# Both batch pairs of a delta-rule attention issued together on TensorE, the second into the other half of PSUM

## The chip, the cores and the metric

The kernel runs on one core of a Trainium2 chip. The metric is the device time of one execution in microseconds (us). Engines are named as in the profile: PE is TensorE (PEld its weight loads), DVE is VectorE, ACT is ScalarE, POOL is GpSimd, SP is SyncE, which only issues DMAs here.

## The reference

An attention with a delta rule, followed by two MLPs on its output. B = 4 batches, H = 8 heads, S = 768 tokens, D = 48.

```python
k_n = k / (norm(k) + 1e-06)
for t in range(S):
    y[:, :, t] = q_t @ state
    v_old = state^T k_t
    state = state + beta_t * outer(k_t, v_t - v_old)
x = y rearranged to 3072 tokens x 384
x = relu(x @ w_in)**2 @ w_out             # d_ff 2048, "MoE1"
x = (silu(x @ w_gate) * (x @ w_val)) @ w_out2   # d_ff 1536, "MoE2"
```

All is float32 (the kernel's large products use a high and a low part in fp32r, three products for one).

## The kernel before

Tokens go in six steps J of 128 tokens of all four batches; a step has two chunks c of 64 tokens. The four batches are two pairs p, and the two batches a of a pair lie on the two halves of the 128 partitions. Within a chunk the recurrence is solved in closed form. The pieces, each a small block of fp32 matmuls for one chunk and one pair, are (with the name of the PSUM tile in the profile):

- gram (`ps_g`, L387/L388): k k^T, 64x64 for each head and batch. From it, masked and scaled by beta on DVE (L457, L458), comes the triangular matrix M, which SP sends to DRAM (`m_out`, L465) and loads back in another layout (`tload`, L470). POOL then inverts 32x32 blocks of it in place, in the tile T (`inv`, L512 and L519), some 40 us for a step. SP sends the result out (`nout`, L546) and back (`nback`, eight DMAs, L561).
- t11, m1, m2 (`tq`, `ps_m`, `ps_x`): the off-diagonal block of the inverse, from transposes on DVE (L612) and two products of 32x32 blocks.
- agram (`ps_a`): q k^T, masked on DVE (L498). ks (`ps_k`): the old state times k, subtracted from V on DVE (L646). u (`ps_u`): the inverse times that. ku (`ps_s`): the change of state. y (`ps_y`, L676/L679): the output, copied by ACT into `ys` (L685).

A matmul of float32 runs as two passes, so a block of 8 heads and 2 batches is 32 matmuls in the trace. The two batches of a pair use the tiles (rows 0-63, columns 0-63) and (rows 64-127, columns 64-127) of TensorE, or, where the layout of the keys makes it so, the two others; two of the four 64x64 tiles are in use at a time, and in m1 and m2 two 32x32 tiles.

Norms of the keys: squares on POOL for the later steps (`sq`, L356), sums on DVE (L360), then a chain of eight small DVE operations (`root`, L371 to L378) that gives `nB`; V is multiplied by it on POOL (`vn`, L319). `v` loads V by SP.

After the attention of step 0, MoE1 of step J runs together with the attention of step C = J + 1. MoE1 of a step is a list of half-slots: nine 128x512 matmuls into `ps_h` (L862), then nine into `ps_y` (L888), and so on. Function `plan(C, P)` names for each of 32 half-slots which pieces of the attention of step C, and which gram pieces of the next step P, follow it; `slot` runs what is due. So the order on PE and on SP is the program's order. DVE's order during MoE1 is the program's order too. On POOL and ACT the compiler's scheduler chooses the order at build time, from when it thinks operands will be there. All engines execute in order. The sum of MoE1 (`ye`) goes to DRAM through DMAs that POOL issues (`y_scr`, L905). MoE2 follows, with no attention beside it.

PSUM: three banks hold MoE1's sums (`ps_a`), two its `ps_h`, and three (`ps_t`) all small blocks of the attention. Tile `xr` has two buffers, shared by M and `ys`; V has two buffers.

Of the kernel before, what the change touches and what calls it, by code (L numbers as in the profile page):

```python
# [8 lines left out]
F32 = mybir.dt.float32  # L9
# [12 lines left out]
def delta_attention_moe_moe2_kernel(  # L22
# [361 lines left out]
    def gram_mm(J, c, p, ps):  # L384
        kt = KT[J, c][:, p]
# [22 lines left out]
    def m0(J, c, p):  # L408
        m = MS[J, c, p]
        nc.vector.scalar_tensor_tensor(out=m, in0=g0.pop((J, c, p)), scalar=-1.0, in1=m, op0=ALU.mult, op1=ALU.mult)  # L410
# [37 lines left out]
    def gram(J, c, p, pool=False):  # L448
        ps = ps_t.tile([128, 8, 64], F32, tag="t", name="ps_g")
        gram_mm(J, c, p, ps)  # L450
        m = ap.tile([128, 8, 64], F32, tag="xr", bufs=XR, name="M")
        mk = mask.unsqueeze(1).to_broadcast([128, 8, 64])
        if pool:
            nc.scalar.activation(out=m, in_=ps, func=ACTF.Copy, scale=-1.0)
            nc.gpsimd.tensor_tensor(m, m, mk, op=ALU.mult)
        else:
            nc.vector.scalar_tensor_tensor(out=m, in0=ps, scalar=-1.0, in1=mk, op0=ALU.mult, op1=ALU.mult)  # L457
        (nc.gpsimd if pool else nc.vector).tensor_tensor(  # L458
            m, m, bB[:, 2 * J + c, p, :].unsqueeze(2).to_broadcast([128, 8, 64]), op=ALU.mult
        )  # L460
        MS[J, c, p] = m
# [27 lines left out]
    def a_mask(J, c, p, eng=None):  # L489
        ps, cs = amm.pop((c, p)), slice(c * 64, (c + 1) * 64)  # L490
        for a in range(2):
            pr = slice(64 * a, 64 * a + 64)
            aq, mk = AQ[p][pr, a, :, cs], mask[pr].unsqueeze(1).to_broadcast([64, 8, 64])
            if eng:
                nc.scalar.activation(out=aq, in_=ps[pr], func=ACTF.Copy)
                eng.tensor_tensor(aq, aq, mk, op=ALU.mult)
            else:
                nc.vector.tensor_tensor(aq, ps[pr], mk, op=ALU.mult)  # L498

    def invert(J, part, parts, eng, pr=slice(0, 128)):  # L500
# [4 lines left out]
        for kk in rows[30 * part // parts:30 * (part + 1) // parts]:  # L505
# [91 lines left out]
    def tr11(J, c, p):  # L597
        t = TD[0][:, p] if J == 0 and c else ap.tile([128, 8, 32], F32, tag="tq", bufs=2, name="tq")
        if J == 0:
            ps = bank(p, [128, 8, 32], "ps_tq")  # L600
            for h in range(8):
                for b0 in (0, 64):
                    nc.tensor.matmul(
                        ps[b0:b0 + 32, h], ND[b0:b0 + 32, 16 * c + 8 * p + h], ident[b0:b0 + 32, b0:b0 + 32],
                        start=True, stop=True,
                    )
            for b0 in (0, 64):
                copy(b0 // 64, t[b0:b0 + 32], ps[b0:b0 + 32])
            t11[c, p] = t
            return  # L610
        for b0 in (0, 64):
            nc.vector.transpose(out=t[b0:b0 + 32], in_=NT[c][p][b0:b0 + 32, :, 0:32])  # L612
        t11[c, p] = t

    def merge1(J, c, p):
        ps = bank(p, [128, 8, 32], "ps_m")
        t = t11[c, p]
        n = NT[c][p]
        for h in range(8):
            for b0 in (0, 64):  # L620
                nc.tensor.matmul(ps[b0 + 32:b0 + 64, h], n[b0:b0 + 32, h, 32:64], t[b0:b0 + 32, h], start=True, stop=True)  # L621
        for b0 in (32, 96):
            copy(b0 // 64, t[b0:b0 + 32], ps[b0:b0 + 32])

    def merge2(J, c, p):
        ps = bank(p, [128, 8, 32], "ps_x")
        n = NT[c][p]
        qq = t11.pop((c, p))
        for h in range(8):
            for b0 in (0, 64):  # L630
                r = slice(b0 + 32, b0 + 64)
                b_ = n[r, h, 32:64] if J else ND[r, 16 * c + 8 * p + h]
                nc.tensor.matmul(ps[b0:b0 + 32, h], qq[r, h], b_, start=True, stop=True)  # L633
        for b0 in (0, 64):
            copy(b0 // 64, n[b0:b0 + 32, :, 32:64], ps[b0:b0 + 32])


    def ks(J, c, p):
        if J == 0 and c == 0:
            return  # L640
        ps = bank(p, [128, 8, 48], "ps_k")
        kt = KT[J, c][:, p]
        for h in range(8):
            nc.tensor.matmul(ps[0:64, h], kt[64:112, h], RS[p][64:112, 0, h], start=True, stop=True)  # L644
            nc.tensor.matmul(ps[64:128, h], kt[0:48, h], RS[p][0:48, 1, h], start=True, stop=True)
        nc.vector.tensor_tensor(VT[J, c][:, p], VT[J, c][:, p], ps, op=ALU.subtract)  # L646

    def uu(J, c, p):
        ps = bank(p, [128, 8, 48], "ps_u")
        for h in range(8):  # L650
            for b0 in (0, 64):
                nc.tensor.matmul(  # L652
                    ps[b0:b0 + 64, h], NT[c][p][b0:b0 + 64, h], VT[J, c][b0:b0 + 64, p, h], start=True, stop=True
                )
        for a in range(2):
            pr = slice(64 * a, 64 * a + 64)
            nc.vector.tensor_tensor(
                RS[p][pr, a], ps[pr], bB[pr, 2 * J + c, p, :].unsqueeze(2).to_broadcast([64, 8, D]), op=ALU.mult
            )

    def ku(J, c, p):
        pk = bank(p, [128, 8, 48], "ps_s")
        for h in range(8):
            nc.tensor.matmul(pk[64:112, h], KB[J, c][0:64, p, h], RS[p][0:64, 0, h], start=True, stop=True)  # L664
            nc.tensor.matmul(pk[0:48, h], KB[J, c][64:128, p, h], RS[p][64:128, 1, h], start=True, stop=True)
        return pk

    def state(p, pk):
        nc.vector.tensor_tensor(RS[p][64:112, 0], RS[p][64:112, 0], pk[64:112], op=ALU.add)
        nc.vector.tensor_tensor(RS[p][0:48, 1], RS[p][0:48, 1], pk[0:48], op=ALU.add)  # L670
# [73 lines left out]
    def do_ku(J, c, p):  # L744
        if (J, c) != (NJ - 1, 1):
            pks[J, c, p] = ku(J, c, p)

        if (J, c) == (0, 0):
            state(p, pks.pop((J, c, p)))

    def do_y(J, c, p):
# [15 lines left out]
        "amm": (lambda J, c, p: a_gram(J, c, p, split=True), 0.8), "amask": (a_mask, 0),  # L767
# [14 lines left out]
    def plan(C, P, pool=(), gram_at=(8, 11, 14, 16), agram_at=(3, 6), norm_at=NRM, t11_at=3, nback_at=4):  # L782
# [8 lines left out]
        for p in range(2):  # L791
            at(0, ("ks", C, 0, p))
            at(t11_at, ("t11", C, 0, p))
            at(5, ("m1", C, 0, p))
            at(7, ("m2", C, 0, p))
            at(agram_at[p], ("agram", C, 0, p))
            at(U0[p], ("u", C, 0, p))
            at(K0[p], ("ku", C, 0, p))
            at(Y0[p], ("y", C, 0, p))
            at(KS1[p], ("ks", C, 1, p))  # L800
            at(15, ("t11", C, 1, p))
            at(18, ("m1", C, 1, p))
# [476 lines left out]
```

## Time and profile before

| what | value |
|---|---|
| three runs | 1131.73, 1134.98, 1136.25 us, median 1134.98 |
| span of the profiled execution, first to last instruction | 1128.7 us |
| PE busy | 1061.7 us, 94% of the span |
| DVE, ACT, POOL busy | 610.4, 381.0, 232.4 us |
| start and attention of step 0, then MoE1 of step 0 with C = 1 | 0 to 215 us |
| MoE1 with the attention of C = 2, 3, 4 | three stretches of about 100 us, to 519 us |
| rest of MoE1 with C = 5, MoE1 of the last step | to 690 us |
| MoE2 | 690 to 1128.7 us |

The profiled execution's own time is given by its span; the median of the runs is 6.3 us above it. Busy times are a share of the whole and average over stages with different limits, so the rows further down go by stage.

### The profile page before, as it was taken

Reading aid. Unit: us, or ns where it says so; the run is one execution under the profiler, and the core shown is the slowest. Engines: PE = TensorE matmul, PEld = TensorE weight load, DVE = VectorE, ACT = ScalarE, POOL = GpSimd, SP = SyncE. Lnnn points to the kernel's source line nnn. Section 1 sums busy time; section 2 is a strip of 40 time slices with the busy share of each in tenths; the row PEclk is TensorE's granted clock in tenths of the full one; section 3 lists DMA queues with packets and bytes.
Section 4 is the critical chain, followed back from the end, with each engine's and each line's share of the span. In section 5 each row is a group of like instructions: output and inputs, shape, how many; then the busy total and the mean of one; then the engine's idle time right before and its main releaser. Section 6 shows DMA issues by size and latency. Waiting matters only on the chain.

```text
span 1128.7 us, 24358 instructions
## 1 busy us (share of the span) xinstructions
PE 1061.7 (94%) x10591; PEld 881.4 (78%) x10591; DVE 610.4 (54%) x1026; ACT 381.0 (34%) x683; POOL 232.4 (21%) x367
## 2 busy tenths in 40 slices
PE   5478879999999999999999999999999999999998
PEld 4376767878888887888888787888888888888887
DVE  5777977465475557545443799333343343333333
ACT  2224744322342233234234786222122121221212
POOL 4258005810851381085000000000000000000000
PEclk8567979999999999999999999999999999999999
DMA  9455304533162353324101565001010010100000
GB/s 298 159 148 155 80 21 100 125 88 86 44 154 56 65 122 90 72 44 106 31 17 57 196 224 168 1 1 56 1 56 1 1 56 1 56 1 1 29 1 28
DMA packets 116922, 84.50 MB, mean 75 GB/s; under 512 B 91472, under 2 KB 95440, under 8 KB 116816
## 3 DMA queue, kind: packets, MB, share of 16 engines
q1 hardware_dynamic: 115616, 77.97, 25.3%
q0 software_dynamic: 1056, 4.72, 1.1%
q8 instruction: 83, 1.36, 0.5%
q10 hardware_dynamic: 144, 0.26, 0.1%
q14 instruction: 23, 0.19, 0.1%
HBM read 61.70 MB, written 21.23 MB: 73 GB/s over the span
## 4 chain that ended last, share of the span: by engine, by line
PE 80%; DVE 8%; issue 3%; POOL 3%; DMA 3%; ACT 2%; SPq 0%; DVEq 0%; POOLq 0%; ACTq 0%
PE ps_h L862 15%; PE ps_y L888 15%; PE ps_o L980 13%; PE ps_g L955 13%; PE ps_v L955 13%; PE ps_u L652 2%; PE ps_g L387 2%; PE ps_a L480 2%; POOL T L519 1%; PE ps_k L644 1%; POOL TMP L512 1%; PE ps_m L621 1%; PE ps_y L676 1%; PE ps_x L633 1%; PE ps_s L664 1%
## 5 line engine op out<-in xcount | busy, mean ns | idle before, releaser
L862 PE MATMUL ps_h<-xh,w 128*128 128x512 f32 (+1 forms) x636 | 204.6, 382 | 3.7 <-DVE w L209 3.1
L888 PE MATMUL ps_y<-hh,w 128*128 128x512 f32 (+1 forms) x606 | 156.0, 393 | 0.0
L955 PE MATMUL ps_g<-x2h,w 128*128 128x512 f32 x432 | 144.8, 389 | 0.0
L955 PE MATMUL ps_v<-x2h,w 128*128 128x512 f32 x432 | 144.7, 389 | 0.0
L959 DVE SCALAR_TENSOR_TENSOR th<-th,ps_g 128x512 f32<-128x512 f32 x72 | 49.4, 687 | 170.6 <-ACT th L958 170.3
L862 PEld LDWEIGHTS ps_h<-xh,w 128*128 128x128 f32 x636 | 117.4, 190 | 27.2 <-DVE w L209 3.9
L865 ACT ACTIVATE r<-ps_h 128x512 f32<-128x512 f32 (+1 forms) x106 | 58.7, 554 | 221.5 <-PE ps_h L862 205.9
L888 PEld LDWEIGHTS ps_y<-hh,w 128*128 128x128 f32 x606 | 109.1, 192 | 22.2
L868 DVE TENSOR_TENSOR r<-r 128x512 f32<-128x512 f32 (+1 forms) x72 | 46.9, 651 | 138.8 <-ACT hh L866 138.4
L862 PE MATMUL ps_h<-xl,w 128*128 128x512 f32 (+1 forms) x318 | 119.1, 374 | 1.8 <-DVE xl L725 1.3
L980 PE MATMUL ps_o<-ph,w 128*128 128x512 f32 x432 | 111.9, 389 | 1.3 <-ACT ye L904 1.3
L958 ACT ACTIVATE th<-ps_g 128x512 f32<-128x512 f32 x72 | 43.0, 597 | 180.1 <-PE ps_g L955 180.1
L512 POOL TENSOR_TENSOR TMP<-T 128x30 f32<-128x30 f32 (+9 forms) x150 | 86.4, 576 | 80.2 <-DMA T<-m_scr 69.2
L980 PEld LDWEIGHTS ps_o<-ph,w 128*128 128x128 f32 x432 | 81.0, 188 | 18.4 <-ACT ye L904 1.7
L519 POOL TENSOR_TENSOR T<-T,TMP 128x30 f32<-128x30 f32 (+9 forms) x150 | 92.4, 616 | 11.4
L955 PEld LDWEIGHTS ps_g<-x2h,w 128*128 128x128 f32 x432 | 81.1, 188 | 17.1 <-issue 0.3
L872 DVE TENSOR_TENSOR hl<-r,hh 128x512 fp32r<-128x512 f32 (+1 forms) x106 | 74.6, 704 | 36.6 <-ACT r L870 30.9
L955 PEld LDWEIGHTS ps_v<-x2h,w 128*128 128x128 f32 x432 | 81.1, 188 | 16.8
L962 ACT ACTIVATE ph<-th 128x512 fp32r<-128x512 f32 x72 | 45.5, 632 | 133.0 <-DVE th L960 133.0
L888 PE MATMUL ps_y<-hl,w 128*128 128x512 f32 (+1 forms) x303 | 83.0, 382 | 5.6 <-DVE hl L872 5.6
L955 PE MATMUL ps_g<-x2l,w 128*128 128x512 f32 x216 | 84.1, 389 | 0.0
L955 PE MATMUL ps_v<-x2l,w 128*128 128x512 f32 x216 | 84.0, 389 | 0.0
(146 smaller groups left out, 1700.9 us busy)
## 6 DMA issues: line engine op xcount, KB each, us to landing
raw<-in_moe_w_out_dram SPq DMA_DIRECT2D x13, 768.0 KB, 7.1
raw<-in_moe_w_in_dram SPq DMA_DIRECT2D x8, 768.0 KB, 12.1
KT<-in_kt_dram SPq DMA_DIRECT2D x12, 448.0 KB, 9.1
m_scr<-M SPq DMA_DIRECT2D x20, 256.0 KB, 2.4
KB<-in_kn_dram SPq DMA_DIRECT2D x12, 384.0 KB, 8.1
AQ<-in_q_dram SPq DMA_DIRECT2D x12, 384.0 KB, 7.0
V<-in_v_dram SPq DMA_DIRECT2D x12, 384.0 KB, 3.8
raw<-in_moe_w_gate_dram SPq DMA_DIRECT2D x6, 768.0 KB, 4.4
```

The costliest lines, as they stand in the source:

```text
L512: eng.tensor_tensor(tmp[:, r0:r1], t_[:, r0:r1, kk:kk + 1].to_broadcast([n, r1 - r0, w]), t_[:, kk:kk + 1, kk + 1:].to_broadcast([n, r1 - ...
L519: eng.tensor_tensor(t_[:, r0:r1, kk + 1:], t_[:, r0:r1, kk + 1:], tmp[:, r0:r1], op=ALU.add)
L862: nc.tensor.matmul(ps, w_[:, kk], x_[:, kk, cols], start=n == 0, stop=n == 3 * KD - 1)
L865: nc.scalar.activation(out=r, in_=ps, func=ACTF.Relu)
L868: nc.vector.tensor_tensor(r, r, r, op=ALU.mult)
L872: eng.tensor_tensor(hl[:, at], r, hh[:, at].bitcast(F32), op=ALU.subtract)
L888: nc.tensor.matmul(acc[f], w_[:, fs], h_, start=first, stop=m == NM1 - 1 and n == 2)
L955: nc.tensor.matmul(ps, w_[:, kk], x_[:, kk], start=n == 0, stop=n == 3 * KD - 1)
L958: nc.scalar.activation(out=th, in_=gp, func=ACTF.Tanh, scale=0.5)
L959: nc.vector.scalar_tensor_tensor(out=th, in0=th, scalar=1.0, in1=gp, op0=ALU.add, op1=ALU.mult)
L962: nc.scalar.activation(out=hh, in_=th, func=ACTF.Copy)
L980: nc.tensor.matmul(o_acc[J][f], w_[:, fs], h_, start=m == 0 and n == 0, stop=m == NM2 - 1 and n == 2)
```

## The change

Every attention piece is now written once for both pairs: `over` issues, head by head, pair 0 and pair 1 and in them both batches. Pair 1 writes swapped halves of its PSUM bank (`blk`, `sub`, `dims`), so that the four products of a head use all four 64x64 tiles (in m1 and m2 four 32x32 tiles). An evacuation of pair 1 whose two halves were one 128-partition operation becomes two of 64 partitions (`parts`): in gram, in ks, in `m0` and in `g_copy` (one of its halves on DVE). The plan places both pairs of a piece in one half-slot; gram of a chunk is placed at half-slots 11 and 14 instead of 8, 11, 14, 16, agram of the first chunk at 4 instead of 3 and 6, u at 9, ku at 12 and 24, ks of the second chunk at 16. The store of M (`m_out`) is issued within gram.

```diff
+    def parts(p):
+
+        if p == 0:
+            return [(slice(0, 128), slice(0, 128))]
+        return [(slice(64 * a, 64 * a + 64), blk(1, a)) for a in range(2)]
...
+    def over(what):
+
         for h in range(8):
-            nc.tensor.matmul(ps[0:64, h], kt[64:112, h], kt[64:112, h], start=True, stop=True)
-            nc.tensor.matmul(ps[64:128, h], kt[0:48, h], kt[0:48, h], start=True, stop=True)
+            for p in range(2):
+                for a in range(2):
+                    what(h, p, a)
+
+    def gram_mm(J, c, pss):
+        def one(h, p, a):
+            k = KT[J, c][KR[a], p, h]
+            nc.tensor.matmul(pss[p][blk(p, a), h], k, k, start=True, stop=True)
+
+        over(one)
...
-    def gram(J, c, p, pool=False):
-        ps = ps_t.tile([128, 8, 64], F32, tag="t", name="ps_g")
-        gram_mm(J, c, p, ps)
-        m = ap.tile([128, 8, 64], F32, tag="xr", bufs=XR, name="M")
+    def gram(J, c):
+        pss = banks([128, 8, 64], "ps_g")
+        gram_mm(J, c, pss)
         mk = mask.unsqueeze(1).to_broadcast([128, 8, 64])
...
+        for p in range(2):
+            m = ap.tile([128, 8, 64], F32, tag="xr", bufs=XR, name="M")
+            for d, r in parts(p):
+                nc.vector.scalar_tensor_tensor(
+                    out=m[d], in0=pss[p][r], scalar=-1.0, in1=mk[d], op0=ALU.mult, op1=ALU.mult
+                )
+            nc.vector.tensor_tensor(
+                m, m, bB[:, 2 * J + c, p, :].unsqueeze(2).to_broadcast([128, 8, 64]), op=ALU.mult
+            )
+            MS[J, c, p] = m
+            m_out(J, c, p)
...
-    def plan(C, P, pool=(), gram_at=(8, 11, 14, 16), agram_at=(3, 6), norm_at=NRM, t11_at=3, nback_at=4):
+    def plan(C, P, gram_at=(11, 14), agram_at=4, norm_at=NRM, t11_at=3, nback_at=4):
...
-            for (c, p), i in zip(((0, 0), (1, 0), (0, 1), (1, 1)), gram_at):
-                at(i, ("gram", P, c, p, *pool), ("mout", P, c, p))
-            at(gram_at[2], ("tload", P, 0))
-            at(gram_at[3], ("tload", P, 1), ("inv", P, 0, 1, nc.gpsimd))
+            for c in range(2):
+                at(gram_at[c], ("gram", P, c), ("tload", P, c))
+            at(gram_at[1], ("inv", P, 0, 1, nc.gpsimd))
             at(11, ("v", P, 0))
```

Two places in the program show what else moves. First SP (all its rows are DMA issues), from the end of the inversion for step C = 3 on. Before, with `T_107` the inverted blocks and `M_4404` the first M of the next step:

```order
L546 DMA n_scr1_92<-T_107 128x1024
L561 DMA NT_101<-n_scr1_92 32x16x32 x8
L465 DMA m_scr0_89<-M_4404 128x8x64
L314 DMA V_4472<-in_v_dram 128x768
L465 DMA m_scr0_89<-M_4508 128x8x64
```

After, with `V_4465` what was `V_4472` (the V of the second chunk of C = 3):

```order
L581 DMA n_scr1_92<-T_107 128x1024
L596 DMA NT_101<-n_scr1_92 32x16x32 x8
L306 DMA V_4465<-in_v_dram 128x768
L499 DMA m_scr0_89<-M_4518 128x8x64
L499 DMA m_scr0_89<-M_4522 128x8x64
```

The load of V stood behind the first store of M and now stands directly behind the returns of the inverse.

Second POOL, around the same place. Before, from the last operations of the inversion to the first of the next one; `sq_4126` and `sq_4129` are the squares of the first chunk's keys of the next step, the DMA rows the two stores of MoE1's sums:

```order
L356 TENSOR_TENSOR sq_4126<-KB_3939 128x384
L512 TENSOR_TENSOR TMP_108<-T_107 128x30
L519 TENSOR_TENSOR T_107<-T_107,TMP_108 128x30
L905 DMA y_scr1_84<-ye_4118 128x768
L905 DMA y_scr1_84<-ye_4122 128x768
L356 TENSOR_TENSOR sq_4129<-KB_3939 128x384
L356 TENSOR_TENSOR sq_4216<-KB_3943 128x384
L356 TENSOR_TENSOR sq_4219<-KB_3943 128x384
L319 TENSOR_TENSOR V_4472<-V_4472,nB_99 128x768
L319 TENSOR_TENSOR V_4512<-V_4512,nB_99 128x768
```

After:

```order
L547 TENSOR_TENSOR TMP_108<-T_107 128x30
L554 TENSOR_TENSOR T_107<-T_107,TMP_108 128x30
L348 TENSOR_TENSOR sq_4140<-KB_3952 128x384
L311 TENSOR_TENSOR V_4465<-V_4465,nB_99 128x768
L965 DMA y_scr1_84<-ye_4132 128x768
L965 DMA y_scr1_84<-ye_4136 128x768
L348 TENSOR_TENSOR sq_4143<-KB_3952 128x384
L348 TENSOR_TENSOR sq_4249<-KB_3956 128x384
L348 TENSOR_TENSOR sq_4252<-KB_3956 128x384
L311 TENSOR_TENSOR V_4529<-V_4529,nB_99 128x768
```

The scaling of the second chunk's V moved from behind all four squares to behind the first one, ahead of both stores and of `sq_4143`. The same move stands at C = 4 (`V_5708`).

## Rows read from the trace of the kernel before

**Rows 1.** Busy time by stretch; columns: stretch, length, each engine, TensorE clock, DMA, GB/s.

```profile
319.20:418.90 99.70, 99.08 (x1340) 81.61 (x1339) 58.73 (x109) 31.71 (x66) 43.10 (x70) 1.00 0.37 89
```

**Rows 2.** Groups by line and shape, whole span, PE: count, busy us, mean ns, idle.

```profile
L652 PE MATMUL ps_u<-V,NT 64*64 64x48 f32 x768 | 29.3, 234 | 2.8 <-issue 2.8
...
L387 PE MATMUL ps_g<-KT 48*64 48x64 f32 x384 | 29.2, 237 | 5.1 <-DMA KT<-in_kt_dram 4.9
```

**Rows 3.** Timeline, PE, where u meets gram; start us, us, engine, line, operation.

```profile
165.06 0.22 PE L387 MATMUL ps_g<-KT 48*64 48x64 f32 x1
...
165.07 0.22 PE L652 MATMUL ps_u<-V,NT 64*64 64x48 f32 x1
...
165.12 0.22 PE L387 MATMUL ps_g<-KT 48*64 48x64 f32 x1
...
165.13 0.22 PE L652 MATMUL ps_u<-V,NT 64*64 64x48 f32 x1
```

**Rows 4.** Timeline, PE: m1 of C = 2, gram's end, a half-slot, m1 of C = 3, 4, 5.

```profile
233.58 0.31 PE L621 MATMUL ps_m<-tq,NT 32*32 32x32 f32 x7
...
273.24 0.22 PE L387 MATMUL ps_g<-KT 48*64 48x64 f32 x1
...
273.40 0.50 PE L862 MATMUL ps_h<-xh,w 128*128 128x512 f32 x1
...
331.86 0.40 PE L862 MATMUL ps_h<-xh,w 128*128 128x512 f32 x1
...
334.04 0.44 PE L621 MATMUL ps_m<-tq,NT 32*32 32x32 f32 x16
...
433.78 0.31 PE L621 MATMUL ps_m<-tq,NT 32*32 32x32 f32 x8
...
532.77 0.25 PE L621 MATMUL ps_m<-tq,NT 32*32 32x32 f32 x4
```

**Rows 5.** Timeline, ACT: the copy of the first pair's y at C = 2.

```profile
264.06 0.60 ACT L685 ACTIVATE ys<-ps_y 128x512 f32<-128x512 f32 x1 [1.90 <-PE ps_y L679]
```

**Rows 6.** Timeline, DVE then POOL: M after the last gram, and the inversion for C = 3.

```profile
275.07 0.69 DVE L458 TENSOR_TENSOR M<-M,bB 128x512 f32<-128x512 f32 x1
...
282.80 0.25 POOL L512 TENSOR_TENSOR TMP<-T 128x30 f32<-128x30 f32 x1 [18.58 <-DMA T<-m_scr]
...
324.14 0.38 POOL L519 TENSOR_TENSOR T<-T,TMP 128x30 f32<-128x30 f32 x1
```

**Rows 7.** Timeline, SP, POOL and DVE behind the inversion, C = 3.

```profile
327.26 4.54 SPq L561 DMA_DIRECT2D NT<-n_scr  x8
...
326.50 0.84 POOL L356 TENSOR_TENSOR sq<-KB 128x384 f32<-128x384 f32 x1
...
327.37 0.55 DVE L360 TENSOR_REDUCE NS<-sq 128x8 f32<-128x384 f32 x1 [1.76 <-POOL sq L356]
...
330.31 0.18 DVE L378 TENSOR_TENSOR bB<-bB,NS 128x16 f32<-128x16 f32 x1
...
330.92 0.42 DVE L872 TENSOR_TENSOR hl<-r,hh 128x256 fp32r<-128x256 f32 x1
...
331.26 0.89 DVE L612 STREAM_TRANSPOSE tq<-NT 32x256 f32<-32x256 f32 x2
...
332.19 1.39 DVE L498 TENSOR_TENSOR AQ<-ps_a,mask 64x512 f32<-64x512 f32 x2
```

**Rows 8.** Timeline, POOL behind the inversion, C = 5, where no squares follow.

```profile
521.79 0.30 POOL L519 TENSOR_TENSOR T<-T,TMP 128x30 f32<-128x30 f32 x1
...
532.85 1.47 POOL L319 TENSOR_TENSOR V<-V,nB 128x768 f32<-128x768 f32 x1 [10.76 <-PE ps_h L862]
...
534.27 1.11 POOL L905 DMA_DIRECT2D y_scr<-ye  x2
```

**Rows 9.** PE at the longest wait, and the clock eight us behind its end.

```profile
147.04 0.28 PE L621 MATMUL ps_m<-tq,NT 32*32 32x32 f32 x3 [8.45 <-issue]
...
154.00:155.00 1.00, 1.00 (x4) 0.76 (x4) 0.97 (x2) 0.00 (x0) 0.00 (x0) 0.69 0.00 0
```

More of the change, by code (lines that the diff above doesn't have):

```diff
@@ L493, in a_mask, with invert @@
             aq, mk = AQ[p][pr, a, :, cs], mask[pr].unsqueeze(1).to_broadcast([64, 8, 64])
[L494 to L500, printed above, removed]
+            nc.vector.tensor_tensor(aq, ps[blk(p, a)], mk, op=ALU.mult)
+    def invert(J, part, n_parts, eng, pr=slice(0, 128)):
         rows = list(range(30, 0, -1))
@@ L504, in invert @@
         n = t_.shape[0]
-        for kk in rows[30 * part // parts:30 * (part + 1) // parts]:
+        for kk in rows[30 * part // n_parts:30 * (part + 1) // n_parts]:
             w = 31 - kk
@@ L609, in tr11 @@
[L609 to L638, printed above, removed]
+        for p in range(2):
+            for b0 in (32, 96):
+                copy(b0 // 64, t11[c, p][b0:b0 + 32], pss[p][sub(p, b0)])
@@ new lines, in merge2 @@
+    def merge2(J, c):
+        pss = banks([128, 8, 32], "ps_x")
+        for h in range(8):
+            for p in range(2):
+                for b0 in (0, 64):
+                    r = slice(b0 + 32, b0 + 64)
+                    b_ = NT[c][p][r, h, 32:64] if J else ND[r, 16 * c + 8 * p + h]
+                    nc.tensor.matmul(pss[p][sub(p, b0), h], t11[c, p][r, h], b_, start=True, stop=True)
+        for p in range(2):
+            t11.pop((c, p))
+            for b0 in (0, 64):
+                copy(b0 // 64, NT[c][p][b0:b0 + 32, :, 32:64], pss[p][sub(p, b0)])
@@ L639, in ks @@
+    def ks(J, c):
         if J == 0 and c == 0:
             return
[L641 to L653, printed above, removed]
-                )
-        for a in range(2):
[L656 to L670, printed above, removed]
+        pss = banks([128, 8, 48], "ps_k")
@@ new lines, in one, with uu @@
+        def one(h, p, a):
+            nc.tensor.matmul(
+                pss[p][blk(p, a), h], KT[J, c][KR[a], p, h], RS[p][KR[a], a, h], start=True, stop=True
+            )
+        over(one)
+        for p in range(2):
+            for d, r in parts(p):
+                v_ = VT[J, c][d, p]
+                nc.vector.tensor_tensor(v_, v_, pss[p][r], op=ALU.subtract)
+    def uu(J, c):
+        pss = banks([128, 8, 48], "ps_u")
+        def one(h, p, a):
+            r = slice(64 * a, 64 * a + 64)
+            nc.tensor.matmul(pss[p][blk(p, a), h], NT[c][p][r, h], VT[J, c][r, p, h], start=True, stop=True)
+        over(one)
+        for p in range(2):
+            for a in range(2):
+                pr = slice(64 * a, 64 * a + 64)
+                nc.vector.tensor_tensor(
+                    RS[p][pr, a], pss[p][blk(p, a)],
+                    bB[pr, 2 * J + c, p, :].unsqueeze(2).to_broadcast([64, 8, D]), op=ALU.mult,
+                )
@@ new lines, in dims, with ku, one, state @@
+    def dims(p, a):
+        o = 64 * (1 ^ a ^ p)
+        return slice(o, o + 48)
+    def ku(J, c):
+        pks_ = banks([128, 8, 48], "ps_s")
+        def one(h, p, a):
+            r = slice(64 * a, 64 * a + 64)
+            nc.tensor.matmul(pks_[p][dims(p, a), h], KB[J, c][r, p, h], RS[p][r, a, h], start=True, stop=True)
+        over(one)
+        return pks_
+    def state(p, pk):
+        for a in range(2):
+            s_ = RS[p][KR[a], a]
+            nc.vector.tensor_tensor(s_, s_, pk[dims(p, a)], op=ALU.add)
```

192 lines of the change are left out of this document (107 added, 85 removed).

## The prediction

> **What bounds the kernel now.** I read the busy time by stretch first, to see where PE is the bound. In the stretch of C = 3, PE works 99.08 of 99.70 us at full clock [rows 1]; C = 2 and C = 4 look alike. So there every microsecond of PE counts, and nothing else does as long as the chains that feed PE keep up. Second, the groups by line, for how much the small products are: u is 768 passes, gram 384 on each of its two lines [rows 2], so 128 of each in one of six steps, and a and k have as many. Third, the timeline where two pieces meet, for the rate of such passes. Fourth, PE's time at each m1, where a step's cycle can be measured: 233.58, 334.04, 433.78 and 532.77 [rows 4], that is 100.46, 99.74 and 98.99 us. Last, the chain from a step's last gram over M, POOL's inversion and the returns to the next m1, with the order of POOL and DVE around it. It decides, since it is nearly as long as PE's work beside it.
>
> Before, gram of C = 2 ends at 273.40 and m1 of C = 3 starts at 334.04, 60.64 us later [rows 4]. In it the inversion ends at E = 324.52, 51.1 us after the gram, and m1 follows 9.5 us after E [rows 4, 6].
>
> **The change part by part.** *Rate of the products.* Gram alone issues its two lines' passes every 0.06 us, so 30 ns a pass. Where u runs out and gram starts, both do so at once: gram at 165.06 and 165.12, u at 165.07 and 165.13 [rows 3]. One uses the tiles (0,0) and (64,64), the other the crossed ones, so all four are at work with each at its own rate. I take 15 ns saved for each 64-wide pass; the other end is no overlap, 0. For s, 48 wide, 11 ns by proportion. For m1 and m2, 16 passes take 0.44 us, of which the last pass alone is some 0.2 [rows 4], so some 16 ns a pass, and I take half of it, 8.
>
> *From m1 to the last gram.* Between these PE has in the new plan 64 passes of u and 128 of gram (192 x 15 = 2.9 us), 64 of s (0.7), 128 of m1 and m2 (1.0). Fewer blocks stand apart: gram's last pass starts at 273.24 and the next large matmul at 273.40 [rows 4], 0.16 in place of 0.06, and I count the same 0.10 on entering; six blocks fewer are 1.2. Work that only changes place: two half-slots, since the last gram goes from half-slot 16 to 14 (331.86 to 334.04 is 2.18 with its border [rows 4], so 4.4), and a block of a and one of k (32 x 30 ns + 0.2 each, 2.4). Against it: the second pair's y now follows the first's directly and writes the bank that ACT still copies, 0.60 [rows 5], with some 0.25 to start; before, s of the second pair stood between. Gram of the second chunk waits alike for the second copy. Together 1.7. Queued behind either is all of PE. So 39.8 (273.40 less 233.58) becomes 39.8 - 2.9 - 0.7 - 1.0 - 1.2 - 4.4 - 2.4 + 1.7 = 28.9.
>
> *From the last gram to E.* DVE makes four 128-wide products for M of both pairs, one of them now in two, where one pair with two stood behind the last gram; an operation is 0.69 [rows 6]. Three more are 2.1, but the subtraction of k no longer stands ahead of them; I take 0.9 later, so E is 52.0 after the gram.
>
> *From E to m1: the part that costs.* SP's rows in the change show V's load directly behind the returns of the inverse, and POOL's rows show the scaling of that V ahead of both `y_scr` stores and of the second square. POOL executes in order. What this order costs can be seen in the kernel before at C = 5, where it occurs with no squares behind it: the inversion ends at 522.09, POOL then stands still until 532.85 for a V that comes behind the eight returns, scales it for 1.47 and issues the two stores in 1.11 [rows 8]. At C = 3 before, V's scaling stood last, and the second square ran at 326.50, right behind the stores. In the new order that square, 0.84 [rows 7], begins at E + 10.76 + 1.47 + 1.11 and ends at E + 14.2. DVE, in order too, has its sum next, and behind it the root: from 327.37 to 330.49, 3.1 [rows 7], so E + 17.3. Behind that stand one pair of r and hl (0.85, from 330.49 to 331.34, where the row of hl ends), so hl, which MoE1's next sums need, comes at E + 18.2; four transposes (two are 0.89), E + 20.0; r and hl of full width (2 x 0.69), E + 21.4; and one pair's masks, 1.39 [rows 6, 7], which free m1's bank: E + 22.8 in place of E + 9.5. Nothing on PE can pass m1 or the sums that need hl, so PE stands for about 13 us.
>
> That stop also costs clock. After the wait of 8.45 us at 147.04 the granted clock is still 0.69 in the slice from 154 [rows 9], on its way from the lower level (1.2 GHz) to the full one. Part of such a time lies before m1 here, where PE waits anyhow; I take 1.5 us, between 0 and 3.5 (half of the seven).
>
> So m1 to m1 is 28.9 + 52.0 + 22.8 + 1.5 = 105.2, at C = 2 to 3 and again at 3 to 4: +4.7 and +5.5. From C = 4 to 5 there are no squares behind the inversion (the row's own 10.7 from E to m1 at C = 5 [rows 4, 8]): 28.9 + 52.0 + 10.7 = 91.6, which is -7.4. PE's own work from gram to m1 would be about 61, and is covered by the chain.
>
> *After m1 of C = 5* there is no gram any more: 256 passes of 64 wide (3.8), s 0.7, m and x 256 x 8 = 2.0, borders 0.6, less 1.7 of waits: -5.4. *Up to m1 of C = 2* DVE and the conversion of weights bound long parts, as PE's wait of 8.45 [rows 9] shows; one step there can gain up to what a steady one does on PE, about 9, or nothing, and the half-clock products of the first step a little more. Ends 0 and -12; I take -5.5, near the middle, since neither has a row of its own. The added 64-wide halves elsewhere (ks, `m0`, `g_copy`) lie on DVE beside PE work in the steady stages, 58.73 of 99.70 [rows 1]; uncovered they would be 0.5 to 0.7 each. MoE2 is not touched.
>
> Sum: -5.5 + 4.7 + 5.5 - 7.4 - 5.4 = -8.1. The span of 1128.7 would be 1120.6; the median of the runs stands 6.3 above the profiled span, so the forecast is 1134.98 - 8.1, about **1127 us**.
>
> **The rivals.** *The block does not bite.* If V lands much earlier, or POOL's square is done in time, m1 follows the inversion at E + 9.5 as before: m1 to m1 is 28.9 + 52.0 + 9.5 = 90.4, so -10.1 and -9.3 in place of +4.7 and +5.5, the rest as above: -37.7, **1097 us**. For it: POOL's work before finished within the time, and the returns may be faster on a quieter queue. Against it: the wait of 10.76 is there word for word at C = 5 [rows 8], and nothing in the change shortens the eight returns that take 4.54 [rows 7].
>
> *The four tiles do not run at once, so it is slower.* Four products of a head come as two tiles in each half of the rows, in turn. If a second tile in the same rows has to wait for the first, the products keep 30 ns a pass; the waits and the block stay. Then 28.9 becomes 33.5, m1 to m1 109.8, +9.3 and +10.1; C = 4 to 5 and the ends come out even: +20, **1155 us**. It decides from the point where the saving of a pass is under some 6 ns of 15, since the block's 26 us then outweighs. For it: the overlap in the rows is two or three passes long [rows 3], at a border, never 32 in a row. Against it: over these passes each pair keeps its 0.06.
>
> The Trainium skill has a rule for this side: by "TensorE: Matmul & The Clock Gate", Part 3, The mechanism, a weight load overlaps matmuls in flight only where its row group differs. By that rule the second pair, in the first one's row groups, would gain nothing, and the time would be that of this rival. The trace leans the other way: u and gram share row groups at 165.06 to 165.13 and neither slows [rows 3].
>
> **How the numbers follow.** I give the likeliest case 0.64, no block 0.20, no four tiles 0.16. The likeliest alone ranges over 1115 to 1139: the start 6 either way, the rate of 32-wide products and the clock 3 each, two blocks of 13 us known to about 2 each. About 0.5%, 5.7 us, is what a measurement can tell from no change: of the likeliest case some 0.6 lies faster than that, 0.33 within, 0.07 slower. So faster 0.38 + 0.20 = 0.58, same 0.22, slower 0.04 + 0.16 = 0.20. The range runs from 1097 to 1148: it leaves out half of the no-block case and most of the no-tiles case.
>
> **What would show it.** Four tiles: blocks of u, gram, a and k of 64 passes in about one microsecond instead of two. The block: at C = 3 and C = 4, POOL idle for some 10 us behind the inversion, ended by V; DVE waiting for a square; a stop of PE of about 13 us ahead of m1 or of the sums before it, with the clock down, and m1 some 75 us behind the last gram; none at C = 2 and C = 5. The y stalls: ps_y waiting for ACT 0.85 us. The forecast is wrong if PE has no stop at C = 3, or if the blocks keep their length.

## The result: slower by 0.7%, and the profile after

The changed kernel takes 1142.16 us (median of six runs, 1138.45 to 1144.72), the kernel before 1134.35 in the same series. The ratio is 1.0074, interval 1.005 to 1.0099. The forecast was 1127: the time lies in the range, but on the other side of the kernel before.

The page's first part of the kernel after, engine busy times and shares, shows that the products did get cheaper: PE had 1061.7 us of work and has 1008.0, in a span that is 9.6 us longer.

```profile
PE 1008.0 (89%) x10591; PEld 825.3 (73%) x10591; DVE 627.6 (55%) x1049; ACT 381.8 (34%) x683; POOL 229.7 (20%) x367
```

The groups by line for the same pieces, to be held against [rows 2], say where. Gram on one line now has all 768 passes; u had 29.3 us for as many and has 16.7:

```profile
L407 PE MATMUL ps_g<-KT 48*64 48x64 f32 x768 | 18.7, 257 | 9.6 <-DMA KT<-in_kt_dram 4.6 <-DVE RS L707 3.6 <-ACT ys L745 1.4
...
L701 PE MATMUL ps_u<-V,NT 64*64 64x48 f32 x768 | 16.7, 238 | 2.9 <-issue 2.6
```

In the timeline of PE a block of both pairs is one row of 64 passes in 1.15 us. The passes of one pair were 30 ns apart [rows 3], so 64 took 1.9.

```profile
360.82 1.15 PE L701 MATMUL ps_u<-V,NT 64*64 64x48 f32 x64
...
366.20 1.16 PE L407 MATMUL ps_g<-KT 48*64 48x64 f32 x64
```

The cycle is read at m1, as in [rows 4]. These are PE's first m1 of C = 2, 3, 4 and 5, each with the matmul of MoE1 that follows the last gram between them:

```profile
240.64 0.25 PE L658 MATMUL ps_m<-tq,NT 32*32 32x32 f32 x4
...
274.51 0.50 PE L922 MATMUL ps_h<-xh,w 128*128 128x512 f32 x1
...
350.69 0.25 PE L658 MATMUL ps_m<-tq,NT 32*32 32x32 f32 x4
...
379.70 0.50 PE L922 MATMUL ps_h<-xh,w 128*128 128x512 f32 x1
...
456.47 0.25 PE L658 MATMUL ps_m<-tq,NT 32*32 32x32 f32 x4
...
485.50 0.50 PE L922 MATMUL ps_h<-xh,w 128*128 128x512 f32 x1
...
549.34 0.25 PE L658 MATMUL ps_m<-tq,NT 32*32 32x32 f32 x6
```

| stretch | before | forecast | after |
|---|---|---|---|
| start to m1 of C = 2 | 233.6 | 228.1 | 240.6 |
| m1 to last gram, C = 2 | 39.8 | 28.9 | 33.9 |
| last gram to m1 of C = 3 | 60.6 | 76.3 | 76.2 |
| m1 to last gram, C = 3 | 39.1 | 28.9 | 29.0 |
| last gram to m1 of C = 4 | 60.7 | 76.3 | 76.8 |
| m1 of C = 4 to m1 of C = 5 | 99.0 | 91.6 | 92.9 |
| m1 of C = 5 to the end | 595.9 | 590.5 | 589.0 |

From the last gram of C = 2 on, every stretch lies within 1.5 us of its forecast. What the forecast missed stands ahead of it: 12.6 us up to m1 of C = 2, and 5 us from there to that gram.

The block that was forecast is there. These are POOL's rows behind the inversion for C = 3 (the counterpart of [rows 7, 8]), then DVE's, then PE's; brackets give the wait ahead and what ended it:

```profile
327.21 0.24 POOL L554 TENSOR_TENSOR T<-T,TMP 128x30 f32<-128x30 f32 x1
327.41 0.83 POOL L348 TENSOR_TENSOR sq<-KB 128x384 f32<-128x384 f32 x1
338.82 1.47 POOL L311 TENSOR_TENSOR V<-V,nB 128x768 f32<-128x768 f32 x1 [10.58 <-DMA V<-in_v_dram]
340.23 1.12 POOL L965 DMA_DIRECT2D y_scr<-ye  x2
341.37 0.84 POOL L348 TENSOR_TENSOR sq<-KB 128x384 f32<-128x384 f32 x1
```

```profile
342.24 0.55 DVE L352 TENSOR_REDUCE NS<-sq 128x8 f32<-128x384 f32 x1 [11.43 <-POOL sq L348]
...
345.78 0.43 DVE L932 TENSOR_TENSOR hl<-r,hh 128x256 fp32r<-128x256 f32 x1
```

```profile
346.27 1.01 PE L948 MATMUL ps_y<-hl,w 128*128 128x256 f32 x3 [10.54 <-DVE hl L932]
```

The inversion ends at E = 327.45. V's scaling begins at E + 11.4 (forecast 10.8), DVE's sum waits 11.43 us for the second square, hl comes at E + 18.8 (18.2), PE has waited 10.54 us for it, and m1 starts at E + 23.2 (22.8). The stretch that holds the wait, by busy time and granted clock:

```profile
346.00:350.00 4.00, 3.73 (x10) 3.12 (x11) 3.81 (x8) 0.00 (x0) 0.00 (x0) 0.50 0.00 0
```

The clock in it is 0.50, the lower of the two levels. From the matmul of hl to m1 it takes 4.42 us here, and 2.62 us for the same matmuls at full clock in the run a_vlate below (437.43 to 440.05), so the clock cost 1.8 us ahead of m1 (forecast 1.5).

Up to m1 of C = 2 the page of waits (engine and line, waited for; us, times, longest) has new rows. All but the last lie at C = 1, where the kernel before had one long wait, of 8.4 us [rows 9]; the last is at C = 2:

```profile
PE ps_a L514 <- DVE NS L352: 4.6, 1, 4.6
...
PE ps_m L658 <- DVE NS L352: 4.4, 1, 4.4
...
PE ps_a L514 <- issue: 4.4, 1, 4.4
...
PE ps_g L407 <- DVE RS L707: 3.6, 1, 3.6
...
PE ps_m L658 <- DVE AQ L533: 3.2, 1, 3.2
```

### The profile page after: what moved, and what is told of

The parts are those of the page before. It is cut to its first block, busy times and chain, and to the rows that moved or that the text cites. A ratio compares the mean times of both kernels' runs of the same rounds, so it can differ in the third digit from the quotient of the medians.

```text
span 1138.3 us, 24409 instructions
## 1 busy us (share of the span) xinstructions
PE 1008.0 (89%) x10591; PEld 825.3 (73%) x10591; DVE 627.6 (55%) x1049; ACT 381.8 (34%) x683; POOL 229.7 (20%) x367
## 4 chain that ended last, share of the span: by engine, by line
PE 51%; DVE 14%; issue 11%; POOL 10%; DMA 9%; ACT 3%; SPq 1%; DVEq 0%; POOLq 0%; ACTq 0%
PE ps_o L1040 13%; PE ps_v L1015 13%; PE ps_g L1015 13%; POOL T L554 5%; PE ps_y L948 5%; PE ps_h L922 5%; POOL TMP L547 4%; DVE raw L180 2%; DMA m_scr<-M 1%; DMA T<-m_scr 1%; DVE raw L185 1%; DMA n_scr<-T 1%; DVE M L488 1%; DVE w L201 1%; DVE f L178 1%
## 5 line engine op out<-in xcount | busy, mean ns | idle before, releaser
L922 PE MATMUL ps_h<-xh,w 128*128 128x512 f32 (+1 forms) x636 | 207.1, 385 | 4.1 <-DVE w L201 3.5
L928 DVE TENSOR_TENSOR r<-r 128x512 f32<-128x512 f32 (+1 forms) x72 | 50.2, 697 | 104.9 <-ACT hh L926 104.6
L948 PEld LDWEIGHTS ps_y<-hl,w 128*128 128x128 f32 x303 | 56.7, 194 | 38.4 <-DVE hl L932 27.3
```

The lines of the kernel that those rows point to most:

```text
L922: nc.tensor.matmul(ps, w_[:, kk], x_[:, kk, cols], start=n == 0, stop=n == 3 * KD - 1)
L928: nc.vector.tensor_tensor(r, r, r, op=ALU.mult)
L948: nc.tensor.matmul(acc[f], w_[:, fs], h_, start=first, stop=m == NM1 - 1 and n == 2)
```

## The experiments

Ratios are to runs of the kernel before on the same chip, with the interval; kernels that build on the changed one say so.

| run | us | ratio, interval |
|---|---|---|
| changed kernel | 1142.2 | 1.0074, 1.005 to 1.0099 |
| a_vlate: V's load later | 1126.1 | 0.9946, 0.993 to 0.9962 |
| b_vearly: kernel before, V's load earlier | 1157.5 | 1.0231, 1.0209 to 1.0252 |
| a_sqsb: squares in T | 1145.0 | 1.0107, 1.0087 to 1.0127 |
| a_both: V later, squares in T | 1129.5 | 0.9979, 0.9962 to 0.9996 |
| a_sqxr: squares on POOL | 1138.5 | 1.0055, 1.0038 to 1.0072 |
| a_vl_sqxr: V later, squares on POOL | 1124.0 | 0.993, 0.9915 to 0.9946 |
| a_vl_pair: V later, pairs one after the other | 1138.2 | 1.0055, 1.004 to 1.0071 |
| a_vl_g16: V later, gram at 16 | 1140.0 | 1.0063, 1.0041 to 1.0086 |
| a_ld2: a_vl_sqxr and keys' load at 16 | 1118.9 | 0.9882, 0.9868 to 0.9895 |
| a_ag6: a_vl_sqxr and agram at 6 | 1121.9 | 0.9908, 0.9895 to 0.9922 |
| a_ge: a_vl_sqxr and gram at 10, 11 | 1115.4 | 0.9845, 0.9829 to 0.986 |
| a_all2: all of these | 1116.6 | 0.9857, 0.9837 to 0.9878 |
| a_sqld: squares on POOL, keys' load at 16 | 1134.7 | 1.0025, 1.001 to 1.0041 |
| a_ge_ld2: a_ge and keys' load at 16 | 1112.8 | 0.9835, 0.9819 to 0.9851 |

**The block, taken away and brought in.**

```diff
-        at(10, ("v", C, 1))
+        at(12, ("v", C, 1))
```

> The changed kernel with the load of the second chunk's V named at half-slot 12 instead of 10, behind the first stores of M on SP; POOL's order has its scaling behind all four squares again. Theory (that scaling, ahead of the second square, holds POOL, DVE and PE at C = 3 and C = 4): m1 follows the last gram after some 61.5 us instead of 76, so about 14.5 us less twice, 1142 - 29 = 1113 us, and no stop of PE over 4 us between 300 and 460. Rival (the stops at C = 3 and 4 come from both pairs taking two PSUM banks at once and from the masks in a row on DVE): little changes, 1137 to 1143 us.

By the ratios it takes 14.5 us less, and the stops at C = 3 and 4 are gone: no wait of PE between 300 and 460 us is longer than 1.8 us. It is about half of what was expected: from the last gram to m1 it takes 67.4, 65.3 and 65.1 us, not 61.5. Against the changed kernel this is 20 us less at C = 3 and 4 together; some 6 of it are lost again in smaller pieces, at the start, from m1 to the last gram, and at C = 5. The 65.3 can be taken apart. PE's gram ends, POOL's inversion begins with the row of 388.60, and m1 follows:

```profile
374.76 0.50 PE L922 MATMUL ps_h<-xh,w 128*128 128x512 f32 x1
```

```profile
388.60 0.26 POOL L547 TENSOR_TENSOR TMP<-T 128x30 f32<-128x30 f32 x1 [10.24 <-DMA NT<-m_scr]
```

```profile
437.43 0.62 PE L948 MATMUL ps_y<-hl,w 128*128 128x256 f32 x3 [1.50 <-DVE hl L932]
...
440.05 0.25 PE L658 MATMUL ps_m<-tq,NT 32*32 32x32 f32 x4
```

The inversion starts 13.8 us behind the gram; in the kernel before it was 10.2 at the same place (9.4 one step earlier [rows 4, 6]). It ends 39.7 later (41.0 before), and m1 follows after 11.7 us (9.5 before). In these 11.7 us PE still waits 1.50 for hl, which DVE makes behind its sums and the root. The first number has its cause in DVE's rows of the changed kernel at C = 2: M is written into the two buffers that ys of the y just ahead still holds until their DMAs are done.

```profile
276.45 0.69 DVE L488 SCALAR_TENSOR_TENSOR M<-ps_g,mask 128x512 f32<-128x512 f32 x1 [2.58 <-DMA xs_scr<-ys]
...
279.09 1.39 DVE L488 SCALAR_TENSOR_TENSOR M<-ps_g,mask 64x512 f32<-64x512 f32 x2 [1.22 <-DMA xs_scr<-ys]
```

The opposite edit, in the kernel before and with nothing else of the change:

```diff
-            at(10, ("v", C, 1))
+            at(7, ("v", C, 1))
```

> The kernel before with the load of the second chunk's V named at half-slot 7 instead of 10, so that it stands directly behind the returns of the inverse; POOL's order then has its scaling ahead of both stores and of the second square at C = 3 and C = 4, as in the changed kernel, and nothing else of the change is in it. Theory: the scaling waits some 10.8 us, PE stops about 13 us ahead of m1 at C = 3 and at C = 4, with 1.5 us of clock each: 1134 + 29 = 1163 us. Rival (the stops need the paired pieces): 1134 to 1138 us.

It takes 25.2 us more. POOL's row at C = 3 has the same wait, and PE waits for hl as in the changed kernel:

```profile
334.43 1.47 POOL L319 TENSOR_TENSOR V<-V,nB 128x768 f32<-128x768 f32 x1 [10.71 <-DMA V<-in_v_dram]
```

```profile
341.87 1.01 PE L888 MATMUL ps_y<-hl,w 128*128 128x256 f32 x3 [10.29 <-DVE hl L872]
```

From the last gram to m1 it takes 72.5 and 74.0 us where it took 60.6: 25.2 together. So the block needs nothing of the four tiles; one load's place on SP, and what the scheduler makes of it on POOL, is enough.

**What the four tiles are worth.**

```diff
-        for h in range(8):
-            for p in range(2):
+        for p in range(2):
+            for h in range(8):
```

> The changed kernel with V at half-slot 12, and the products of pair 0 issued ahead of those of pair 1 in each piece, so that two tiles work at a time; plan, banks, swapped halves and split evacuations stay. Theory (the four tiles are the gain): a pass takes 30 ns again, some 8 to 10 us more of PE in a step, of which the slack of 4 us before m1 hides a part: 4 to 6 us a step in C = 2 to 5 and a few at the start, 1126 + 22 = 1148 us. Rival (with the chains as they are now PE's products are not the bound): 1126 to 1130 us.

With V late in both, two tiles at a time cost some 12 us (1.0055 against 0.9946): neither 22 nor nothing. The timeline has 64 passes of u in 1.88 us again instead of 1.15, so the tiles do run at once; from m1 to the last gram it is 32.8 instead of 29.3 to 30.9 us, while from the gram to m1 the chain hides most of it (66.2 against 65.3 at C = 3).

```profile
361.22 1.88 PE L701 MATMUL ps_u<-V,NT 64*64 64x48 f32 x64
```

**Gram's place.**

```diff
-    def plan(C, P, gram_at=(11, 14), agram_at=4, norm_at=NRM, t11_at=3, nback_at=4):
+    def plan(C, P, gram_at=(11, 16), agram_at=4, norm_at=NRM, t11_at=3, nback_at=4):
```

> The changed kernel with V at half-slot 12, and the second chunk's gram at half-slot 16 instead of 14. In the profile with V at 12, the inversion starts 13.8 us after that gram, 9.4 before the change: M is written into the buffers that ys of the y just ahead still holds until its DMA is done. Theory (M waits for that DMA): at 16 the DMAs are done, the inversion follows 10 to 11 us after the gram, and what the later place costs (two half-slots, 4.4 us) is given back: 1124 to 1129 us. Rival (the added DVE operations make the 13.8): it stays 13 to 14 us, and the time rises by some 3 x 4 us, to 1136 to 1139.

The inversion now starts 10.0 us behind the gram (387.06 to 397.01), and m1 comes 61.2 to 61.6 us after it at C = 2 and 3: M did wait for ys. Yet the time rose by 13 us, so the price was misjudged. Counted from m1 the gram ends 11 us later and not 4.4; 3 us of this are a wait, since it now stands right behind ks in the same half-slot and its second bank waits for DVE's subtraction:

```profile
385.98 1.15 PE L407 MATMUL ps_g<-KT 48*64 48x64 f32 x60 [3.01 <-DVE V L694]
```

**The slow start: banks at C = 1.** In the changed kernel a piece takes two of the three banks at once, and the squares of step 2 (ACT) lie in the same banks until DVE has summed them.

```diff
-                sq = ps_t.tile([128, 8, 48], F32, tag="t", name="ps_sq")
+                sq = T.rearrange("p a b -> p (a b)")[:, DM * p:DM * (p + 1)].rearrange("p (h d) -> p h d", h=8)
```

> The changed kernel with the squares of the keys of step 2, the only ones that lie in the attention's three PSUM banks once MoE1 runs, put into SBUF (into T, which is free there). Theory for the slow start (at C = 1 a piece of both pairs needs two of three banks and waits for DVE's sums of the squares that hold them, 4.6 and 4.4 us in the profile): the two waits go, m1 of C = 1 comes some 6 to 9 us earlier, and as what follows is a chain to m1 of C = 2 the whole time falls by 5 to 8 us, 1134 to 1137. Rival (DVE's own order with the conversions of weights in it sets m1 of C = 1, and the banks only take the blame): 1140 to 1143 us.

> Both edits together in the changed kernel: the second chunk's V at half-slot 12 and the squares of step 2 in SBUF. Theories: the gains add, as one lies ahead of m1 of C = 2 and the other behind it: 1142 - 29 - 6 = 1107 us, 2.4% below the kernel before. Rivals: with only the V part right 1113, with only the squares right 1136, with neither 1142.

Neither gained: alone the edit gives 1.0107 against 1.0074, with intervals that overlap, and with V late 0.9979 against 0.9946. This edit tells nothing on the banks, because it brought a wait of its own. With a free place to write, ACT's squares moved ahead of MoE1's activations and waited for the keys, and DVE for ACT:

```profile
122.26 0.69 DVE L932 TENSOR_TENSOR hl<-r,hh 128x512 fp32r<-128x512 f32 x1 [11.37 <-ACT r L930]
```

So the squares went to POOL, which is idle there, in the buffers of M:

```diff
-                sq = ps_t.tile([128, 8, 48], F32, tag="t", name="ps_sq")
+                sq = ap.tile([128, 8, 64], F32, tag="xr", bufs=XR, name="sqx")[:, :, 0:48]
...
-            if startup or J < FN:
+            if startup:
```

> The changed kernel with the squares of step 2's keys made on POOL, which is idle there, into two SBUF buffers (those of M and ys) instead of on ACT into the attention's PSUM banks. The earlier try with T put an ACT wait of 11 us ahead, since ACT's squares moved in front of MoE1's activations and waited for the keys; POOL has nothing else to do there. Theory (at C = 1 pieces of both pairs need two of three banks that these squares hold): the waits of 4.6 and 4.4 us on DVE's sums go, m1 of C = 1 ends 5 to 7 us earlier, and the time is 1135 to 1138. Rival (DVE with the weight conversions sets it): 1141 to 1144 us, and m1's end at C = 1 stays within 2 us.

> The same squares, with the second chunk's V at half-slot 12: both causes taken away. Theory: 1126 - 6 = 1120 us, 1.1% below the kernel before. Rival: 1126 us as with the V part alone.

In a_sqxr m1 of C = 1 begins at 143.61 instead of 151.70 and ends at 150.83 instead of 157.50. Its first passes go at once; the rest waits for a bank, in the changed kernel for the sums of the squares and now for the masks of a. The two rows are of the changed kernel, then of a_sqxr:

```profile
156.44 1.06 PE L658 MATMUL ps_m<-tq,NT 32*32 32x32 f32 x60 [4.42 <-DVE NS L352]
```

```profile
149.76 1.07 PE L658 MATMUL ps_m<-tq,NT 32*32 32x32 f32 x60 [5.49 <-DVE AQ L533]
```

Not all of the 6.7 us are the banks': MoE1's first matmul comes 3.2 us earlier too (95.28 against 98.47), and the edit lies behind it. Counted from that matmul, m1 of C = 1 ends after 59.0 to 63.0 us in the four profiles with the squares in the banks (the changed kernel, a_vlate, a_vl_g16, a_vl_pair), and after 53.6 to 57.4 us in the eight with the squares on POOL; in the kernel before it is 54.8. So the banks cost m1 of C = 1 some 4 us or more.

But m1 of C = 2 stays (241.04 against 240.64), and the time falls by some 2 us only, less than the intervals tell apart. SP's rows of a_sqxr show the next wait: the store of the inverse issues 6.5 us earlier than in the changed kernel (230.24 there), yet the returns follow 12.6 us behind it; in the kernel before, 6.4 (222.27 to 228.66).

```profile
220.36 0.59 SPq L301 DMA_DIRECT2D AQ<-in_q_dram  x1
...
222.75 0.42 SPq L290 DMA_DIRECT2D KB<-in_kn_dram  x1
223.22 0.44 SPq L294 DMA_DIRECT2D KT<-in_kt_dram  x1
223.70 0.43 SPq L581 DMA_DIRECT2D n_scr<-T  x1
236.30 4.05 SPq L596 DMA_DIRECT2D NT<-n_scr  x8
```

The keys' and q's loads, 2.4 MB named at half-slot 26 (two of q with 384 KB, two of the keys with 384 and two with 448), used to be issued some 6 us ahead of that store and now stand directly ahead of it. The returns keep their distance from the first of these loads rather than from the store: 15.9 us here (220.36 to 236.30), 15.4 in the kernel before, 14.5 in the changed one, and 14.5 to 17.4 in all twelve profiles with the six loads together, while from the store to the returns it is anything from 5.5 to 13.9.

```diff
-            at(26, *loads(P + 1))
+            at(16, loads(P + 1)[0])
+            at(26, loads(P + 1)[1])
```

> The changed kernel with the squares of step 2 on POOL and the first keys' load at half-slot 16, V still at 10: only what concerns the time up to m1 of C = 2. Theory (the loss there is a sum of three waits: the banks at C = 1, the load queue ahead of the inverse's return, and some 2 to 3 us at the start where DVE is the bound): m1 of C = 2 comes at 235 to 238 us instead of 240.6, and the time is 1133 to 1137 us. Rival (m1 of C = 2 is set by something not touched): 1138 to 1142 us.

> On top of V at half-slot 12 and the squares of step 2 on POOL: the load of the first chunk's keys of the step after next is named at half-slot 16, not 26 with the rest. With the squares moved, m1 of C = 1 came 8 us earlier and the inversion for C = 2 ended 7 us earlier, but m1 of C = 2 hardly moved: the store of the inverse took 8 to 12.6 us to come back, against 6 before, behind 2 MB of loads issued just ahead. Theory (that queue): with 0.8 MB of it earlier, the store and returns are 3 to 5 us faster at C = 1 to 2, m1 of C = 2 comes at some 233 us, and the time falls from 1124 to 1120 us. Rival (DVE with its conversions sets m1 of C = 2): 1123 to 1125.

In a_sqld m1 of C = 2 comes at 237.54 and the time is 1134.7, both as expected, 0.5% less than the changed kernel. In a_ld2 the returns follow 3.9 us behind the store, and 12.0 us behind the first of the four loads that are left there:

```profile
218.99 0.60 SPq L301 DMA_DIRECT2D AQ<-in_q_dram  x1
...
227.08 0.34 SPq L581 DMA_DIRECT2D n_scr<-T  x1
230.97 4.24 SPq L596 DMA_DIRECT2D NT<-n_scr  x8
```

The time of a_ld2 fell as expected, but its profile does not bear out the reason given: m1 of C = 2 is at 237.16 against 237.25 in a_vl_sqxr, since in this run the store itself came 2.8 us later (224.30 there), and the cycle of C = 2 is shorter (96.7 against 99.3). One profile of each can't settle it, as m1 of C = 2 differs by some 2 us between profiles of the same code (a_ge, with the code of a_vl_sqxr up to there, has 239.28).

By the times the two edits together give 5.5 us with V at 10 (a_sqld against the changed kernel) and 7.2 with V late (a_ld2 against a_vlate), both clear of the intervals. The profiles place m1 of C = 2 as follows:

| profiles | m1 of C = 2 |
|---|---|
| kernel before; b_vearly | 233.6; 235.0 |
| changed kernel; with V late (a_vlate, a_vl_g16) | 240.6; 242.2, 242.5 |
| squares on POOL (a_sqxr); with V late (a_vl_sqxr, a_ge) | 241.0; 237.3, 239.3 |
| both edits (a_sqld; a_ld2, a_all2, a_ge_ld2) | 237.5; 237.2, 236.0, 238.9 |

By the means the two edits take back some 4 of 7.5 us, and with V late the squares do nearly all of it. The queue is as long in the kernel before (15.4 us). So it is not a loss that the change brought, but holds back what the squares set free; whether the load's earlier place gains in the kernel before as well was not tried.

Of the other 3 a part stands ahead of MoE1. Its first matmul comes at 95.22 and 95.90 in the kernel before and b_vearly, and at 95.28 to 99.34 in the changed kernel and its thirteen versions, 98.47 in the changed one itself. These rows run up to that matmul, in the kernel before, then in the changed one:

```profile
0.00:95.22 95.22, 56.61 (x1856) 54.19 (x1856) 68.39 (x159) 25.94 (x55) 46.00 (x65) 0.66 0.61 189
```

```profile
0.00:98.47 98.47, 45.00 (x1856) 40.30 (x1856) 73.27 (x166) 26.51 (x55) 48.04 (x68) 0.64 0.60 185
```

For the same 1856 passes PE's work fell by 11.6 us, while DVE's rose by 4.9. Of these, 3.8 are the split halves: M has 6 operations there instead of 4 (4.14 us for 2.58), NT 14 for 12 (12.72 for 11.18), V 5 for 4 (3.65 for 2.94). DVE is almost full towards the end of the stretch, with 14.62 of the 15 us from 80 to 95 before and 14.50 after. That the halves cause the later start was not tried by itself. With the pairs one after the other (a_vl_pair) the matmul comes at 97.32, within the spread of the others, so no sign is seen that PE's rate counts there.

**Better places.** Three more versions place agram behind m1, so that m1 doesn't wait for masks (a_ag6), gram ahead of y (a_ge), and all edits together (a_all2, whose places are these):

```diff
-    def plan(C, P, gram_at=(11, 14), agram_at=4, norm_at=NRM, t11_at=3, nback_at=4):
+    def plan(C, P, gram_at=(10, 11), agram_at=6, norm_at=NRM, t11_at=3, nback_at=4):
```

> On top of V at half-slot 12 and the squares of step 2 on POOL: agram of the first chunk at half-slot 6, behind m1, for C = 2 to 5. Both pairs' a ahead of m1 take two of the three banks, so m1 waits for four masks on DVE (3.2 us at C = 2) and comes 11.7 us after the inversion's end, 9.5 before the change. Theory: m1 no longer waits, 2 to 3 us less in each of three cycles, 1124 - 7 = 1117 us. Rival (m1 waits for the returns of the inverse and the transposes alone): 1123 to 1125.

> On top of V at half-slot 12 and the squares of step 2 on POOL: gram at half-slots 10 and 11 instead of 11 and 14, ahead of y, for the steps 3 to 5. With V out of the way a cycle is 94 to 97 us of which PE works 89; the rest is the chain from gram over M and the inversion to m1, 65 us, lengthened by 4.4 since M waits for the buffers of ys. Theory (the chain sets the cycle): gram 6 to 7 us earlier and no wait for ys, so cycles of 90 to 91 and 1124 - 12 = 1112 us. Rival (the four M share two buffers, each waits for the store of the one before, and y then waits for M): no gain, 1122 to 1130.

> All of it: V at half-slot 12, squares of step 2 on POOL, first keys' load at 16, agram at 6, gram at 10 and 11. Theory: PE bounds the steps at 89 to 91 us and the start is 4 us shorter: 1124 - 16 - 4 = 1104 us, 2.4% below the kernel before. Rival (each of the moves finds the same wait behind another): 1115 to 1124.

> The version with V at half-slot 12, squares of step 2 on POOL, gram at half-slots 10 and 11, and the first keys' load at 16. Theory (what the load's place gave alone, 5 us, lies ahead of the grams' part): 1115 - 5 = 1110 us, 2% below the kernel before. Rival (with gram early the inversion ends earlier and the loads no longer matter): 1114 to 1116 us.

a_ag6 gave 2 us of the 7 expected, within the intervals of nothing. m1's wait for masks went and C = 2 is shorter (31.7 us from m1 to the last gram, 34.7 in a_vl_sqxr), but m1 still begins 12.4 and 11.7 us after the end of the inversion for C = 3 and 4. So the masks are not what delays it there. By the ratios a_ge gave 9.6 of 12 (its profile is 5.6 us shorter), although not as expected: its cycles of C = 2 and 3 are 97.7 and 98.4 us, no shorter than in a_vl_sqxr (99.3, 97.5), and that of C = 4 is 91.4 against 96.5. a_all2 is no better than a_ge, as its rival had it, and a_ge_ld2's 1112.8 lies within a_ge's interval. The best versions are 1.5 to 1.7% below the kernel before; which chain bounds their cycles of 96 to 98 us, with PE busy 91.5 of 98.4 in a_ge, is open.

## Why the prediction was wrong

*The rate of the products* was right: 15 ns a pass, all four tiles at once. The rival without overlap is out, and so is the strict reading of the Trainium skill's rule in "TensorE: Matmul & The Clock Gate", Part 3, The mechanism, that a load of weights overlaps only across row groups: here both pairs share them, and 64 passes take 1.15 us.

*The block at C = 3 and 4* was right in place and mechanism. Its size, 76.2 and 76.8 us from the last gram to m1 against 76.3 forecast, is in part luck. The forecast let the inversion start 0.9 us later behind the gram than before; at C = 3 it starts 4.0 later (13.4 for 9.4), since M waits for the buffers of ys, which the sum did not have. The inversion then took 39.5 us where it had taken 41.7, so E came at 52.9 for 52.0, and m1 followed after 23.2 us where 22.8 and 1.5 for the clock were forecast. Taking the block out of the changed kernel and putting it into the kernel before both moved the time the right way, by 14.5 and 25 us. That the first is less than the second was not foreseen: even without the block the chain is 65 us long and not 61.5, by M's wait for the buffers and by 2 us more from E to m1. The rival "the block does not bite" put 1097 us on its absence; without the block the time is 1126.

*The step that failed* is "Up to m1 of C = 2 ... I take -5.5, near the middle, since neither has a row of its own". It measured +7.1, and 12.6 us of error are more than the whole forecast of -8. The reason given for a gain was that PE's products there shrink too. They did, by 11.6 us up to MoE1's first matmul alone, and that matmul still came 3.3 us later, in a stretch whose end DVE fills (14.50 of the 15 us from 80 to 95). The range from 0 to -12 had no room for a loss, though the change takes two banks at once where three are shared with the squares, and adds halves on DVE, which by the text's own words bounds long parts of that stretch. The runs showed in its place the waits for banks (4 us or more at m1 of C = 1) and a later start of MoE1 beside 3.8 us more of halves on DVE. The banks are shown by taking the squares out of them, with the keys' load moved so that the queue does not eat the gain: some 4 of the 7 us. The cause of the rest stays open.

*From m1 to the last gram at C = 2* was mis-sized by 5 us: 33.9 for 28.9. m1 waits 3.2 us there for masks, since a of both pairs now stands ahead of it and holds two banks, and behind that wait the granted clock is 0.57 from 244 to 248 us. At C = 3 and 4 the block hides that wait, and the term fits (29.0). Of the waits behind ys, y's eight were 0.74 us each and gram's 0.5, forecast 0.85 for either.

*After m1 of C = 5* the change was -6.9 us for a forecast of -5.4.

From m1 of C = 3 to the end the forecast was -7.3 us and the measure -7.0. The sign was lost ahead of it: in the term that had no rows, and in one that was worked out from rows but left out the wait for the masks.

## What to carry to other kernels

Making the bound engine's work cheaper moves the bound: 54 us less work on TensorE came out as 8 us more time, because a chain over DVE, DMA and POOL was nearly as long as TensorE's own work before and got longer by the same change, and because the start lost time too. With one load put back behind the stores, the same products made the kernel 0.5% faster than before. Pairing work to fill an engine also pairs its claims on buffers: count banks and shared tiles piece by piece, in the stage where most others use them too, and give such a stage's term a range with a loss in it. When code that names DMAs moves, look at what a scheduler then does on another engine with what the DMA brings.

## What the runs showed of the hardware

Four 64x64 fp32 products in all four tiles run at twice the rate of two (a pass every 15 ns against 30), also where pairs share row groups: 64 passes take 1.15 us, and 1.88 us with the same instructions in another order. A store of 0.5 MB (128 x 1024 floats) right behind 2.4 MB of loads took 12.6 us until what waits for it could issue, and 5.9 to 6.4 us when it was issued some 6 us behind the last of them; counted from the first load's issue it was 14.5 to 17.4 us in twelve profiles. With 0.8 MB of the loads moved ahead it was 11.5 to 12.4 us in four. MoE1's first matmul varies by up to 4 us between profiles of kernels with nearly the same code up to there (95.28 to 99.34).
